# A decode-step kernel whose last weight rows come mid-run: w2's seventh rows in 13 transfers to three DMA engines' partitions, the residual by one product, w2's rest in four parts

## The chip, the cores and the metric

The kernel runs on one core of a Trainium2 chip. A core has a matrix engine (PE, whose weight loads the profile lists apart as PEld), a vector engine (DVE), an activation engine (ACT), a general engine (POOL) and a queue engine (SP) that here only issues transfers. Sixteen DMA engines move data between the memory of the chip (HBM) and the core's buffer of 128 partitions. Each engine runs its own list of instructions in order and waits where an operand is not ready.

The metric is the device time of one execution in microseconds (us), the median of several runs. Lower is better.

## What is computed

One decode step for a batch of 8: a layer norm of x, attention with a key and value cache of 8192 positions, and beside it a dense layer with the Mish activation. Both results and x are added. All numbers are float32.

```python
xn = _layernorm(x)
# attention: 32 query heads, 8 key/value heads of 128, 8 x 8192 positions
q = (xn @ wq) ...
scores = einsum("bhqd,bhkd->bhqk", q, k) * (Dh ** -0.5)
o = einsum("bhqk,bhkd->bhqd", softmax(scores), v)
att = o @ wo
# dense layer: 512 -> 1792 -> 512
h = xn @ w1 + b1
act = h * tanh(softplus(h))
ffn = act @ w2
return x + att + ffn
```

The two caches are 537 MB of the 561 MB that are read, so nearly all of the work is to bring them in once.

## The kernel before

**Units.** The work is cut into 32 units, j = 0 to 31. Unit j = 8m + b holds batch element b and the pair m of key/value heads. Its keys (kT) and its values (v) are one transfer of 8 MB each, 64 KB to each of the 128 partitions. For each unit the program writes, in this order: `scores(j)` (64 products of PE into the bank S), `softmax(j)`, `values(j - 1)` (64 products into the bank O with the values of the unit before), and `turn(j)`, which turns the exponentials of unit j into the weights `pt8` that `values(j)` reads. Unit 0 also holds `mish`, the whole first half of the dense layer: 32 + 4 passes of PE, then a row of DVE instructions that ends with the activations `aT` (lines 418 to 468). They are read only at the very end.

**Places in the buffer.** One tile `kv` holds all that streams in. Values come to its first 16384 columns (V_AT). Keys come by turns to K_AT[0] = 16384 and K_AT[1] = 24576, both 16384 columns long, so that the second half of the one place is the first half of the other. The keys of unit j + 1 can therefore start once unit j is done with the half that both share; `scores` takes that half first (argument `first`), and the load of the next keys is written between its two halves (line 558). The first weight w1 and everything that `mish` works on lie in K_AT[0] as well, so that the keys of unit 2 (line 558, in unit 1) have to wait for both: the end of `mish`, and the first half of the scores of unit 1, whose keys lie in K_AT[1]. The values of unit 1 have to wait for `values(0)`.

**Order.** The program sets the order by hand: each engine runs its instructions in the order in which the program writes them. All large transfers are issued by SP. SP waits for the place to be free, issues, and goes on to the next one. The query weights wq (four transfers of 2 MB into the tile `ws`) come between: the first at the start, the others in units 4, 12 and 20. From the end of unit 23 on `ws` has no other use than the residual: POOL loads x into its first 128 columns as `xres`, in 16 transfers of two rows each, in units 23 to 30 (line 544).

**The end.** After the last values come four transfers of wo (2 MB each, line 592) and w2 in three parts, 2 MB, 1 MB and 512 KB (line 603). A row of w2_rows belongs to one partition and holds seven pieces of 1024 columns; the parts are the pieces 0 to 3, 4 and 5, and 6. PE adds wo's products (`outputs`) and the first part's (`down_wide`) into the bank A, four groups of rows for four slices of the work; ACT copies A to the buffer (line 615); the parts two and three go to the bank H (`down`), and four products with `bsel` (line 618) add up A's four groups into H as well. DVE adds `xres` (line 627), and SP stores the result.

Of the kernel before, what the change touches and what calls it, by code (L numbers as in the profile page):

```python
# [24 lines left out]
G = 4  # L25
NH = 2
TG = SK // (NH * G) // P
BW = 1024
# [4 lines left out]
Q = P // G  # L33
# [17 lines left out]
W2R = 7  # L51
# [12 lines left out]

LOAD_Q, MAKE_Q, SPREAD_Q = 4, 5, 7

CUTS = tuple((g, lo, lo + 2) for g in range(G) for lo in range(0, B, 2))


@with_exitstack  # L70
def kernel(
# [21 lines left out]
    ws = const.tile([P, CC * BW], F32, name="ws")  # L93
# [13 lines left out]
    lsum = const.tile([P, B, H2], F32, name="lsum")  # L107
# [16 lines left out]
    qsel = const.tile([P, P], F32, name="qsel")  # L124
    oW = const.tile([P, NP, WOR, 2, B], F32, name="oW")
    qr = const.tile([P, DI, H2 * B], F32, name="qr")
    xres = ws[:, :P]
    oT = const.tile([P, 2, H2, B], F32, name="oT")
    aT = const.tile([P, 2 * W2R, B], F32, name="aT")
    pt8 = const.tile([P, HALF, PL * TL, H2], F32, name="pt8")  # L130
# [18 lines left out]
    x_sb, xc, sq = (low[:, i * D : (i + 1) * D] for i in range(3))  # L149
# [13 lines left out]
    for d in range(2):  # L163
        nc.vector.tensor_copy(
            perm.rearrange("p (d k c h) -> p d k c h", d=2, c=2, h=REP)[:, d],
            ident.rearrange("p (c d k h) -> p d k c h", c=2, d=2, h=REP)[:, d],
        )
    nc.vector.reduce_sum(
        gsum, ident.rearrange("p (x g q) -> p g x q", g=4, q=PP), axis=AX.XY
    )  # L170
# [5 lines left out]
    for d in range(2):  # L176
# [3 lines left out]
            axis=AX.XY,  # L180
# [39 lines left out]
    nc.vector.tensor_scalar(st[:, 6:7], st[:, 7:8], -0.5, 1.5, op0=ALU.mult, op1=ALU.add)  # L220
    nc.vector.tensor_mul(st[:, 4:5], st[:, 6:7], st[:, 5:6])
    nc.vector.tensor_scalar(xc, xc, st[:, 4:5], None, op0=ALU.mult)
    for c in range(CC):
        nc.tensor.transpose(M[:, c * B : (c + 1) * B], xc[:, c::CC], ident[:B, :B])
    nc.vector.tensor_copy(xn4.rearrange("p c b -> p (c b)"), M[:, 0:32])
# [192 lines left out]
    def mish(w1_t, b1_sb, flat):  # L418
        hp = H[:, :FG]
        for i in range(W1R):  # L420
            for n in range(2):
                nc.tensor.matmul(  # L422
                    hp[Q * n : Q * n + 2 * B, :],
                    xnT[:, i].rearrange("p h b -> p (h b)"),
                    w1_t[:, i, n * FG : (n + 1) * FG],
                    start=(i == 0),
                    stop=False,
                )
        for n in range(2):
# [24 lines left out]
        act = one  # L454
        half = FG // 2
        for e in range(2):
            nc.vector.tensor_mul(
                act.rearrange("p (i a e l) -> p e a l i", a=2, e=2, i=W2R)[:, e],
                h[:, half * e : half * (e + 1)].rearrange("p (a l i) -> p a l i", a=2, i=W2R),
                t1[:, half * e : half * (e + 1)].rearrange("p (a l i) -> p a l i", a=2, i=W2R),  # L460
            )
        turned = flat[:, 5 * FG : 6 * FG]
        nc.vector.transpose(turned, act)
        for h in range(2):
            nc.vector.tensor_copy(
                aT[64 * h : 64 * (h + 1)],
                turned[:64].rearrange("p (j q) -> p j q", q=Q)[:, :, h * B : (h + 1) * B],
            )


    TURN = {}

    def turn_masked(m):

        nc.vector.tensor_mul(oT[:, m % 2], oT[:, m % 2], rt.rearrange("p b h -> p h b"))
        om = TURN[m] = work.tile([P, 512], F32, name="e")[:, : WOR * H2 * B]
        nc.vector.tensor_mul(
# [18 lines left out]
    def outputs(m, t):  # L496
        w = t.rearrange("p (i h f) -> p i h f", i=WOR, h=2)
        for h in range(2):
            for i in range(WOR):
                nc.tensor.matmul(  # L500
                    A[Q * i : Q * i + B, :],
                    oW[:, m, i, h, :],
                    w[:, i, h],
                    start=(m == 0 and h == 0),
                    stop=False,
                )

    def down_wide(lo, hi, w):
        for j in range(2 * lo, 2 * hi):
            at = (j - 2 * lo) * D  # L510
            nc.tensor.matmul(
                A[Q * (j % G) : Q * (j % G) + B, :],
                aT[:, j, :],
                w[:, at : at + D],
                start=False,
                stop=(j >= 2 * hi - G),
            )

    def down(lo, hi, w, first):
        for j in range(2 * lo, 2 * hi):  # L520
            for g in range(G):
                at = (j - 2 * lo) * D + g * P
                nc.tensor.matmul(  # L523
                    H[Q * g : Q * g + B, :P],
                    aT[:, j, :],
                    w[:, at : at + P],
                    start=(first and j == 2 * lo),
                    stop=(j == 2 * W2R - 1),
                )


# [7 lines left out]
    spread()  # L539
    key_weights(0)  # L540

    def residual(g, lo, hi):

        nc.gpsimd.dma_start(  # L544
            xres[Q * g + lo : Q * g + hi, :], x[lo:hi, g * P : (g + 1) * P]
        )

    v_t = {}
    for j in range(UNITS):
        b = j % B  # L550
# [12 lines left out]
        spreads = more and b == SPREAD_Q  # L563
        if j + 1 < UNITS and not spreads:
            key_weights(j + 1)
        if j > 0:
            os = values(j - 1, v_t.pop(j - 1))
        late = j // B - 1 if b == 1 and j > B else None
        if late is not None:
            turn_masked(late)  # L570
        if j + 1 < UNITS:
            v_t[j] = load_unit(v, j, V_AT)
            if spreads:
                spread()
                key_weights(j + 1)
        for cut in CUTS[2 * (j - 23) : 2 * (j - 22)] if j >= 23 else ():
            residual(*cut)
        if j == 0:
            mish(w1_t, b1_sb, kv[:, W1_AT : W1_AT + 6 * FG])
        if more and b == LOAD_Q:  # L580
            load_q(j // B + 1)
        if more and b == MAKE_Q:
            qT = project(j // B + 1)
            mask_queries(qT)
        turn(j, late)
        if j > 0:
            merge(j - 1, os)
# [3 lines left out]
    for m in range(NP):  # L591
# [3 lines left out]
            .rearrange("u p f -> (u p f)")  # L595
            .rearrange("(p f) -> p f", p=P),
        )
    w2_rows = w2.rearrange("j p f -> (j p) f").rearrange("(q i) f -> q (i f)", i=W2R)
    w2_t = []
    parts = ((0, 4), (4, 6), (6, 7))  # L600
    for lo, hi in parts:
        t = kv[:, W2_AT + lo * BW : W2_AT + hi * BW]
        nc.sync.dma_start(t, w2_rows[:, lo * BW : hi * BW])
# [7 lines left out]
    turn_rows(NP - 1)  # L611
    outputs(NP - 1, w_o[NP - 1])
    down_wide(*parts[0], w2_t[0])
    a_sb = work.tile([P, 512], F32, name="e")
    nc.scalar.copy(a_sb, A)
    down(*parts[1], w2_t[1], True)
    for g in range(G):
        nc.tensor.matmul(
            H[Q * g : Q * g + B, :P],
# [47 lines left out]
```

## Time and profile before

| | |
|---|---|
| median of 3 runs | 1312.17 us (1312.1 to 1312.31) |
| the profiled execution | 1313.53 us, of which the profile shows a span of 1310.3 us |
| read from HBM | 561.03 MB, 428 GB/s over the span |
| PE busy | 907.7 us (69%) |
| DVE busy | 407.4 us (31%) |
| ACT and POOL busy | 41.8 us (3%) and 10.1 us (1%) |
| mean granted PE clock | 0.848 |

Times in the profile are counted from the start of the span. A page of the profile gives the busy time of each engine, then the span in 40 slices, then the DMA queues, then the chain of waits that ended last, followed back from the end. Other views list the instructions in order of time ("timeline": start, duration, engine, line, operation, and in brackets how long the engine stood idle before it and what ended that), the busy time in chosen stretches ("windows"), and the transfers with the time from issue to landing. "L314" is line 314 of the kernel; `x64` is a group of 64 instructions, and a float32 product of PE is two passes, so that 32 products show as 64.

### The profile page before, as it was taken

The page shows a single profiled execution, that of the slowest core. Times are in us where ns is not written, and L with a number is a line of the kernel's source. Part 1 is how long each engine was busy: PE and PEld are TensorE (multiplying, and loading weights), DVE is VectorE, ACT ScalarE, POOL GpSimd, SP SyncE. Part 2 cuts the span into 40 slices and gives each one's busy share as a digit, 9 for nine tenths or more (in the row PEclk, how much of TensorE's full clock was granted, in tenths as well). Part 3 has the DMA queues.
Part 4 walks back from the last instruction along what each step waited for, and adds up shares of the span by engine and source line. Part 5 has one row for each costly group of instructions (what it writes and reads, how often), then busy time and mean ns, then how long its engine had stood idle before and what let it go on. Part 6 is the DMA issues. An engine that isn't in the chain of part 4 may idle for free.

```text
span 1310.3 us, 10389 instructions
## 1 busy us (share of the span) xinstructions
PE 907.7 (69%) x4568; PEld 269.2 (21%) x4568; DVE 407.4 (31%) x881; ACT 41.8 (3%) x96; POOL 10.1 (1%) x24
## 2 busy tenths in 40 slices
PE   4967866768767567777668766687576668657667
PEld 1212221212212112222112212122121112212112
DVE  3363132331333333123331332322233331233330
ACT  1000000000000000000000000000000000000000
POOL 0000000000000000000000000011000000000000
PEclk9979887888888888887798788798887898887788
DMA  9999999999999999999999999999999999999997
GB/s 404 444 427 437 431 433 427 437 440 431 433 431 435 425 441 425 441 426 439 429 433 433 431 437 425 444 421 441 425 437 433 435 429 437 431 436 427 437 417 312
DMA packets 11668, 561.75 MB, mean 429 GB/s; under 512 B 1724, under 2 KB 1888, under 8 KB 2024
## 3 DMA queue, kind: packets, MB, share of 16 engines
q1 hardware_dynamic: 11088, 561.06, 99.2%
q8 instruction: 35, 0.57, 0.2%
q0 software_dynamic: 512, 0.02, 0.0%
q10 hardware_dynamic: 24, 0.02, 0.0%
q14 instruction: 9, 0.07, 0.0%
HBM read 561.03 MB, written 0.07 MB: 428 GB/s over the span
## 4 chain that ended last, share of the span: by engine, by line
DMA 73%; PE 23%; DVE 2%; ACT 0%; issue 0%; SPq 0%; DVEq 0%
DMA kv<-in_v 71%; PE o L393 20%; DMA kv<-in_w 3%; PE s L314 1%; PE h L250 1%; PE h L422 0%; DVE kv L452 0%; DVE tr L363 0%; PE h L523 0%; DVE wk L297 0%; DVE pt L379 0%; DVE y L373 0%; DVE nm L326 0%; ACT L216 0%; DVE ws L270 0%
## 5 line engine op out<-in xcount | busy, mean ns | idle before, releaser
L314 PE MATMUL s<-kv,wk 128*64 128x512 f32 x2048 | 512.9, 665 | 247.5 <-DMA kv<-in_kT 244.8
L393 PE MATMUL o<-kv,pt 128*32 128x512 f32 x2048 | 269.6, 686 | 46.5 <-DMA kv<-in_v 46.5
L314 PEld LDWEIGHTS s<-kv,wk 128*64 128x64 f32 x2048 | 157.5, 154 | 583.1 <-issue 327.3
L326 DVE TENSOR_REDUCE nm<-s 128x1 f32<-128x512 f32 x32 | 22.1, 692 | 547.7 <-PE s L314 547.7
L393 PEld LDWEIGHTS o<-kv,pt 128*32 128x32 f32 x2048 | 70.4, 123 | 219.5 <-issue 178.8
L363 DVE STREAM_TRANSPOSE tr<-x 128x512 f32<-128x512 f32 x128 | 79.8, 681 | 0.1
L401 DVE TENSOR_SCALAR os<-o,isel 128x128 f32<-128x128 f32 x32 | 11.2, 351 | 220.2 <-PE o L393 220.2
L297 DVE TENSOR_TENSOR wk<-qr,mask 128x512 f32<-128x512 f32 x64 | 62.5, 1019 | 5.7 <-ACT qr L286 5.7
L379 DVE SCALAR_TENSOR_TENSOR pt<-tr,gsum,y 64x256 f32<-64x256 f32 x128 | 56.2, 478 | 1.7
L345 ACT ACTIVATE e<-s,nmx 128x512 f32<-128x512 f32 x32 | 22.0, 688 | 1053.1 <-DVE nmx L342 1053.1
L373 DVE SCALAR_TENSOR_TENSOR y<-tr,gsum,y 128x512 f32<-128x512 f32 x64 | 48.4, 756 | 2.3
L350 PE MATMUL x<-e,perm 128*128 128x512 f32 x64 | 36.0, 644 | 0.0
L403 DVE SCALAR_TENSOR_TENSOR os<-o,isel,os 128x128 f32<-128x128 f32 x96 | 33.7, 351 | 3.4
L250 PE MATMUL h<-ws,xn 128*8 128x512 f32 x64 | 31.7, 642 | 0.0
L327 PE MATMUL m<-ident,nm 128*1 128x128 f32 x32 | 8.7, 273 | 29.3 <-DVE nm L326 29.3
L410 PE MATMUL m<-ident,os 128*128 128x128 f32 x32 | 10.3, 323 | 22.2 <-DVE os L403 12.2
L371 DVE TENSOR_SCALAR y<-tr,gsum 128x512 f32<-128x512 f32 x32 | 24.1, 754 | 1.1
L338 PE MATMUL m<-ident,nx 1*128 1x1 f32 x32 | 7.0, 219 | 24.1 <-DVE nx L334 24.1
L346 DVE TENSOR_SCALAR lsum<-rsel,l 128x8 f32<-128x8 f32 x32 | 7.4, 231 | 30.3 <-ACT e L345 30.3
L544 POOL DMA_DIRECT2D ws<-in_x x16 | 8.4, 527 | 901.9 <-PE h L250 870.8
L331 DVE TENSOR_REDUCE nr<-m 1x4 f32<-1x64 f32 x64 | 11.0, 207 | 11.7 <-PE m L327 11.7
L350 PEld LDWEIGHTS x<-e,perm 128*128 128x128 f32 x64 | 9.5, 188 | 23.7 <-issue 21.7
(107 smaller groups left out, 152.7 us busy)
## 6 DMA issues: line engine op xcount, KB each, us to landing
ws<-in_wq SPq DMA_DIRECT2D x4, 2048.0 KB, 34.3
kv<-in_wo SPq DMA_DIRECT2D x4, 2048.0 KB, 24.2
kv<-in_w SPq DMA_DIRECT2D x1, 3584.0 KB, 22.1
kv<-in_w SPq DMA_DIRECT2D x1, 2048.0 KB, 34.7
kv<-in_w SPq DMA_DIRECT2D x1, 1024.0 KB, 36.7
kv<-in_kT SPq DMA_DIRECT2D x32, 29.8
kv<-in_v SPq DMA_DIRECT2D x32, 30.1
kv<-in_w SPq DMA_DIRECT2D x1, 512.0 KB, 37.4
```

Of the source, the lines that this page charges most:

```text
L250: nc.tensor.matmul(H[:B, :], xn4[:, c, :], w[:, c, d * 512 : (d + 1) * 512], start=(c == 0), stop=(c == CC - 1),)
L297: nc.vector.tensor_mul(w[:, :, d], q[:, :, d].to_broadcast([P, DI, NH * G, REP]), mask[:, d * NH * G : (d + 1) * NH * G] .rearrange("p (o ...
L314: nc.tensor.matmul(S[64 * c : 64 * (c + 1), :], w[:, i].rearrange("p d k h -> p (d k h)"), kk[:, i, c, :], start=(part == 0 and n == 0), s ...
L326: nc.vector.tensor_reduce(nm, S, axis=AX.X, op=ALU.max, negate=True)
L345: nc.scalar.activation(e, S, AF.Exp, bias=nmx, accum_out=l)
L350: nc.tensor.matmul(X, perm, e, start=True, stop=True)
L363: nc.vector.transpose(tr.rearrange("p (l t) c -> p t l c", t=TL)[:, tl], X.rearrange("p (t o q l) -> p t l o q", t=TL, o=1, q=PP)[:, tl].t ...
L371: nc.vector.tensor_scalar(y, kinds[:, 0], gsum[:, 0:1], None, op0=ALU.mult)
L373: nc.vector.scalar_tensor_tensor(y, kinds[:, g], gsum[:, g : g + 1], y, op0=ALU.mult, op1=ALU.add)
L379: nc.vector.scalar_tensor_tensor(pt8[half, c, :, d * REP : (d + 1) * REP], kinds[half, 3, :, c * REP : (c + 1) * REP], gsum[half, 3:4], y[ ...
L393: nc.tensor.matmul(O[Q * q : Q * (q + 1), :], pt8[:, c, TL * l : TL * (l + 1), :].rearrange("p t h -> p (t h)"), vt[:, 512 * n : 512 * (n ...
L403: nc.vector.scalar_tensor_tensor(os, O[:, DH * i : DH * (i + 1)], isel[:, i : i + 1], os, op0=ALU.mult, op1=ALU.add)
```

## The change

w2's pieces 0 to 5 still come at the end, now in four parts: 1 MB, 1 MB, 512 KB, 512 KB. The seventh piece (`late_rows`, 128 rows of 4 KB) comes mid-run through ACT's queue into `ws`, in 13 transfers: five in units 16 to 18, eight in units 24 to 27. Twelve of them have three rows of partitions as their outer dimension (partition p, p + 4 and p + 8, with two or four pieces of 4 KB to each), 120 of the 128 rows in all; the thirteenth brings the last 8 rows to eight partitions. Since several rows of w2 now lie in one partition, the activations that belong to them have to be moved to those partitions: `deal_early` does it right behind `mish` in unit 0, with a mask `kmask` and one product with a selection matrix `esel`, into the new tile `aE`. `early_products` multiplies them in units 19 and 29 into the bank A. The residual is now a product of the identity with x at the start, the first one into A; the 16 POOL transfers are gone. Line numbers of the changed kernel are those of the diff's new side, 80 more at the end.

```diff
+LEAD, LS, LK = 3, 4, 4
+SPAN, SLOTS = LEAD * LS, LK + 2
+LATE = 2 * SPAN * LK
+REST = LATE + 2 * SPAN
+EARLY_AT = {16: (8, 10), 17: (10, 12), 18: (12, 13), 24: (0, 2), 25: (2, 4), 26: (4, 6), 27: (6, 8)}
+PRODUCE_AT = {19: (LK, SLOTS, 2 * Q), 29: (0, LK, Q + SPAN)}
...
-    xres = ws[:, :P]
+    esel = const.tile([P, 2 * Q], F32, name="esel")
+    kmask = const.tile([P, SLOTS], F32, name="kmask")
+    aE = const.tile([2 * Q, SLOTS, 2, B], F32, name="aE")
...
+    nc.vector.memset(esel, 0.0)
+    for u in range(2):
+        nc.vector.reduce_sum(
+            esel[:, Q * u : Q * u + SPAN].rearrange("p (e s) -> p e s", e=LEAD),
...
+    nc.vector.tensor_add(kmask[:, LK : LK + 1], kmask[:, LK : LK + 1], lsum[:, 0, :1])
     nc.vector.reduce_sum(
         gsum, ident.rearrange("p (x g q) -> p g x q", g=4, q=PP), axis=AX.XY
...
+    nc.tensor.matmul(A[:B, :], ident[:B, :B], x_sb, start=True, stop=False)
...
+    def deal_early():
+
+        last = work.tile([P, 512], F32, name="e")[:, : SLOTS * 2 * B]
+        nc.vector.tensor_mul(
+            last.rearrange("p (k c) -> p k c", k=SLOTS),
+            aT[:, 2 * W2R - 2 :]
+            .rearrange("p (o e) b -> p o (e b)", o=1)
+            .to_broadcast([P, SLOTS, 2 * B]),
+            kmask.rearrange("p (k o) -> p k o", o=1).to_broadcast([P, SLOTS, 2 * B]),
+        )
+        nc.tensor.matmul(
+            M[: 2 * Q, 192 : 192 + SLOTS * 2 * B], esel, last, start=True, stop=True
+        )
+        nc.scalar.copy(
+            aE.rearrange("p k e b -> p (k e b)"),
+            M[: 2 * Q, 192 : 192 + SLOTS * 2 * B],
+        )
...
-    def residual(g, lo, hi):
-
-        nc.gpsimd.dma_start(
-            xres[Q * g + lo : Q * g + hi, :], x[lo:hi, g * P : (g + 1) * P]
-        )
+    w2_rows = w2.rearrange("j p f -> (j p) f").rearrange("(q i) f -> q (i f)", i=W2R)
+    late_rows = w2_rows[:, (W2R - 1) * BW :]
+
+    def early(n):
+
+        if n < 2 * LS:
+            ks, (u, s), q = LK, divmod(n, LS), n * LK * LEAD
+        else:
+            ks, u, s = 2, 0, n - 2 * LS
+            q = LATE + s * ks * LEAD
+        if n < 3 * LS:
+            p = Q * u + s
+            rows = slice(p, p + (LEAD - 1) * LS + 1, LS)
+            nc.scalar.dma_start(
+                ws[rows, : ks * BW].rearrange("e (k f) -> e k f", k=ks),
+                late_rows[q : q + ks * LEAD].rearrange("(k e) f -> e k f", e=LEAD),
+            )
+        else:
+            nc.scalar.dma_start(ws[Q : 2 * Q : LS, :BW], late_rows[REST:])
+
+    def early_products(lo, hi, rows):
+
+        for n in range(2 * lo, 2 * hi):
+            k, e = divmod(n, 2)
+            at = (n - 2 * lo) * D
+            nc.tensor.matmul(
+                A[Q * (n % G) : Q * (n % G) + B, :],
+                aE[:rows, k, e],
+                ws[:rows, at : at + D],
+                start=(lo > 0 and n % G > 0),
+                stop=False,
+            )
...
-        for cut in CUTS[2 * (j - 23) : 2 * (j - 22)] if j >= 23 else ():
-            residual(*cut)
+        if j in PRODUCE_AT:
+            early_products(*PRODUCE_AT[j])
+        for n in range(*EARLY_AT.get(j, (0,))):
+            early(n)
         if j == 0:
             mish(w1_t, b1_sb, kv[:, W1_AT : W1_AT + 6 * FG])
+            deal_early()
...
-    parts = ((0, 4), (4, 6), (6, 7))
+    parts = ((0, 2), (2, 4), (4, 5), (5, 6))
...
     down_wide(*parts[0], w2_t[0])
+    down_wide(*parts[1], w2_t[1])
     a_sb = work.tile([P, 512], F32, name="e")
     nc.scalar.copy(a_sb, A)
-    down(*parts[1], w2_t[1], True)
+    down(*parts[2], w2_t[2], True)
...
-    down(*parts[2], w2_t[2], False)
+    down(*parts[3], w2_t[3], False)
     res = work.tile([P, DH], F32, name="os", bufs=1)
-    nc.vector.tensor_add(res, H[:, :P], xres)
+    nc.vector.tensor_copy(res, H[:, :P])
```

PE around units 0 and 1, before: `s` are the scores, `m` the transposes of the softmax, `h` the products of `mish`, `x` the first product of `turn(0)`.

```order
L314 MATMUL s<-kv,wk 64x512 x32
L327 MATMUL m<-ident,nm 1x128
L338 MATMUL m<-ident,nx 128x1
L422 MATMUL h<-kv 16x448 x16
L430 MATMUL h<-kv 16x448 x2
L350 MATMUL x<-e,perm 128x512
L314 MATMUL s<-kv,wk 64x512 x32
```

The same place in the changed program:

```order
L346 MATMUL s<-kv,wk 64x512 x32
L359 MATMUL m<-ident,nm 1x128
L370 MATMUL m<-ident,nx 128x1
L454 MATMUL h<-kv 16x448 x16
L462 MATMUL h<-kv 16x448 x2
L513 MATMUL m<-e,esel 64x96
L382 MATMUL x<-e,perm 128x512
L346 MATMUL s<-kv,wk 64x512 x32
```

One product stands between the last product of `mish` and the scores of unit 1; its operand `e` is written by the DVE row below. DVE at the end of `mish` in the changed program (`kv` is the work space of `mish`, `tr`, `y` and `pt_99` belong to `turn(0)`):

```order
L484 RECIPROCAL kv<-kv 128x448
L485 TENSOR_TENSOR kv<-kv 128x448
L489 TENSOR_TENSOR kv<-kv 128x2x16x7 x2
L495 STREAM_TRANSPOSE kv<-kv 128x448
L497 COPY aT<-kv 64x112 x2
L506 TENSOR_TENSOR e<-aT,kmask 128x96
L395 STREAM_TRANSPOSE tr<-x 128x16x32 x4
```

Only L506 is new there, behind the copy to `aT`; at the head of DVE's list ten instructions for `esel` and `kmask` are new, ahead of the other constants. PE at the end of the program, before (`a` and `h` are the banks A and H):

```order
L500 MATMUL a<-kv,oW 8x512 x8
L511 MATMUL a<-kv,aT 8x512 x8
L523 MATMUL h<-kv,aT 8x128 x16
L618 MATMUL h<-e,bsel 8x128 x4
L523 MATMUL h<-kv,aT 8x128 x8
```

and in the changed program, where half of the first group of H's products is gone:

```order
L550 MATMUL a<-kv,oW 8x512 x8
L561 MATMUL a<-kv,aT 8x512 x8
L573 MATMUL h<-kv,aT 8x128 x8
L698 MATMUL h<-e,bsel 8x128 x4
L573 MATMUL h<-kv,aT 8x128 x8
```

More of the change, by code (lines that the diff above doesn't have):

```diff
@@ L65 @@
 LOAD_Q, MAKE_Q, SPREAD_Q = 4, 5, 7
-CUTS = tuple((g, lo, lo + 2) for g in range(G) for lo in range(0, B, 2))
+LEAD, LS, LK = 3, 4, 4
[4 more added lines that the diff above has]
+PRODUCE_AT = {19: (LK, SLOTS, 2 * Q), 29: (0, LK, Q + SPAN)}
 @with_exitstack
@@ L167 @@
         )
+    nc.vector.memset(esel, 0.0)
+    for u in range(2):
+        nc.vector.reduce_sum(
+            esel[:, Q * u : Q * u + SPAN].rearrange("p (e s) -> p e s", e=LEAD),
+            ident[:, :LATE].rearrange("p (u s k e) -> p u e s k", u=2, s=LS, k=LK)[:, u],
+            axis=AX.X,
+        )
+    sums = lsum.rearrange("p b h -> p (b h)")[:, :SPAN]
+    nc.vector.reduce_sum(
+        sums.rearrange("p (e s) -> p e s", e=LEAD),
+        ident[:, LATE:REST].rearrange("p (s k e) -> p e s k", s=LS, k=2),
+        axis=AX.X,
+    )
+    nc.vector.tensor_add(esel[:, :SPAN], esel[:, :SPAN], sums)
+    nc.vector.tensor_add(esel[:, Q::LS], esel[:, Q::LS], ident[:, REST:])
+    for at, lo, hi in ((0, 0, LATE), (LK, LATE, REST)):
+        ks = LK if at == 0 else 2
+        nc.vector.reduce_sum(
+            kmask[:, at : at + ks],
+            ident[:, lo:hi].rearrange("p (x k e) -> p k x e", k=ks, e=LEAD),
+            axis=AX.XY,
+        )
+    nc.vector.reduce_sum(lsum[:, 0, :1], ident[:, REST:], axis=AX.X)
+    nc.vector.tensor_add(kmask[:, LK : LK + 1], kmask[:, LK : LK + 1], lsum[:, 0, :1])
     nc.vector.reduce_sum(
@@ L468, in mish @@
             )
+    def deal_early():
[13 more added lines that the diff above has]
+            M[: 2 * Q, 192 : 192 + SLOTS * 2 * B],
+        )
     TURN = {}
@@ L503, in outputs @@
                     w[:, i, h],
-                    start=(m == 0 and h == 0),
+                    start=False,
                     stop=False,
@@ L515, in down_wide @@
                 start=False,
-                stop=(j >= 2 * hi - G),
+                stop=(j >= 2 * parts[2][0] - G),
             )
@@ L527, in down @@
                     start=(first and j == 2 * lo),
-                    stop=(j == 2 * W2R - 1),
+                    stop=(j == 2 * W2R - 3),
                 )
@@ L540 @@
     key_weights(0)
-    def residual(g, lo, hi):
-        nc.gpsimd.dma_start(
-            xres[Q * g + lo : Q * g + hi, :], x[lo:hi, g * P : (g + 1) * P]
-        )
+    w2_rows = w2.rearrange("j p f -> (j p) f").rearrange("(q i) f -> q (i f)", i=W2R)
[12 more added lines that the diff above has]
+                late_rows[q : q + ks * LEAD].rearrange("(k e) f -> e k f", e=LEAD),
+            )
+        else:
[10 more added lines that the diff above has]
+                stop=False,
+            )
     v_t = {}
@@ L597 @@
         )
-    w2_rows = w2.rearrange("j p f -> (j p) f").rearrange("(q i) f -> q (i f)", i=W2R)
     w2_t = []
-    parts = ((0, 4), (4, 6), (6, 7))
+    parts = ((0, 2), (2, 4), (4, 5), (5, 6))
     for lo, hi in parts:
```

## The prediction

> **What bounds the kernel now.** First the page: the slices of the span, the queues, the chain.
>
> ```profile
> DMA  9999999999999999999999999999999999999997
> DMA packets 11668, 561.75 MB, mean 429 GB/s; under 512 B 1724, under 2 KB 1888, under 8 KB 2024
> q1 hardware_dynamic: 11088, 561.06, 99.2%
> q8 instruction: 35, 0.57, 0.2%
> ...
> DMA 73%; PE 23%; DVE 2%; ACT 0%; issue 0%; SPq 0%; DVEq 0%
> ```
>
> The sixteen DMA engines are busy from the first slice to the last but one. Every byte of caches and weights passes once, at 429 GB/s. PE stands in the chain, but always in turn with a transfer that was queued long before, so making PE faster or slower moves nothing until SP issues a transfer too late. So three things set the time: whether the stream ever runs dry, which DMA engine ends last, and what follows the last byte.
>
> The end, in the view by windows (PE, PEld, DVE, ACT, POOL busy, PE clock, DMA share, GB/s):
>
> ```profile
> 1297.00:1298.00 1.00, 0.59 (x8) 0.23 (x12) 0.12 (x1) 0.20 (x1) 0.00 (x0) 1.00 1.01 422
> 1298.00:1303.00 5.00, 2.17 (x24) 0.34 (x16) 0.00 (x0) 0.00 (x0) 0.00 (x0) 1.00 0.55 233
> ...
> 1304.00:1305.00 1.00, 0.92 (x13) 0.28 (x13) 0.00 (x0) 0.37 (x1) 0.00 (x0) 0.50 0.20 82
> ```
>
> The share falls from 1.01 to 0.55 at 1298 and stays there for five us: 9 of 16 is 0.56. Seven engines are done; nine go on, the last to about 1305.4. Each had the same number of bytes. The single packets of the trace, put into chains (each starts as the one ahead ends), say why: a code load of PE (35 on q8, one per 37 us) holds one engine up by some 1.5 us, and they go round among the nine late ones.
>
> **The stall that I expect.** The new product with `esel` (L513 of the change) reads what DVE makes of `aT`, the last result of `mish`. PE runs in order, and behind this product stand unit 0's first product of `turn`, all scores of unit 1 and `values(0)`. Rows of the timeline of before:
>
> ```profile
> 48.22 0.33 SPq L141 DMA_DIRECT2D kv<-in_v  x1
> ...
> 57.12 1.13 PE L350 MATMUL x<-e,perm 128*128 128x512 f32 x2
> ...
> 58.18 13.95 PE L314 MATMUL s<-kv,wk 128*64 128x512 f32 x64
> ...
> 68.74 0.44 DVE L465 COPY aT<-kv 64x112 f32<-64x112 f32 x2
> ...
> 69.25 0.33 SPq L141 DMA_DIRECT2D kv<-in_kT  x1
> ...
> 76.00 0.69 DVE L326 TENSOR_REDUCE nm<-s 128x1 f32<-128x512 f32 x1
> ...
> 78.06 8.73 PE L393 MATMUL o<-kv,pt 128*32 128x512 f32 x64
> ...
> 95.63 15.37 PE L314 MATMUL s<-kv,wk 128*64 128x512 f32 x64 [6.87 <-DMA kv<-in_kT]
> 104.17 0.33 SPq L141 DMA_DIRECT2D kv<-in_kT  x1
> ```
>
> In before PE starts unit 1's scores at 58.18, beside `mish` on DVE. SP issues unit 2's keys at 69.25, when `aT` is done; the first half of the scores, for which they also wait, had long ended. In the change both stand in one row. Step by step:
>
> ```profile
> 3.08 0.28 DVE L168 TENSOR_REDUCE gsum<-ident 128x4 f32<-128x128 f32 x1
> ...
> 6.08 0.67 DVE L209 TENSOR_REDUCE st<-kv 8x1 f32<-8x512 f32 x1
> ...
> 402.74 0.43 DVE L477 TENSOR_TENSOR e<-oT,usel 128x256 f32<-128x256 f32 x1
> 403.22 0.70 PE L487 MATMUL m<-e,qsel 128*128 128x256 f32 x2 [1.23 <-DVE e L477]
> ```
>
> - Ten more DVE constants stand ahead of the norm of x. Fourteen small ones take 3.08 to 6.08, so 0.21 each: 2.1 us. The way from there to `aT` is one chain (norm, queries, key weights, scores 0, `mish`), so `aT` comes at 71.3, not 69.2.
> - Mask product on DVE 0.3, new product 0.4 (their likes above, twice as wide and more, take 0.43 and 0.70), L350 1.2: the scores of unit 1 start at 73.2, fifteen us later.
> - Their first half takes 7.0 (half of 13.95) if PE runs warm, 8.5 (95.63 to 104.17, where SP waited for just this) after an idle gap. I take 7.9. SP can issue unit 2's keys at 81.1.
>
> ```profile
> 95.00:97.00 2.00, 1.37 (x4) 0.53 (x6) 0.29 (x1) 0.00 (x0) 0.00 (x0) 0.50 1.21 524
> ...
> 99.00:101.00 2.00, 2.00 (x12) 0.60 (x10) 0.00 (x0) 0.00 (x0) 0.00 (x0) 1.00 0.98 426
> ```
>
> After 6.9 us without work the granted clock was 0.50 here and 1.00 again from 99. The gap in the change is 12 us, so the same is due; the product and L350 use up some of the slow time, hence 7.9. The Trainium skill, "TensorE: Matmul & The Clock Gate", section "What's actually happening", says that half speed comes after an idle window of about 3.4 us and ends after as much sustained work. This trace agrees; by that rule the first half is an estimated 7.0 + (3.4 - 1.6) / 2 = 7.9 as well, since the product and L350 fill 1.6 of the slow time, and the sum below stays; with a PE that stayed warm it would be 0.9 lower.
>
> Does the stream last that long? The values of unit 0 were issued at 48.22, in time, and 2 us later still are. Unit 2's keys land in before at 95.6 (L314 waits for them); 8.39 MB at 429 GB/s is 19.55 us, and some 0.4 goes from the last byte to the waiting engine: so the data ahead of them end at 75.6. The packet chains give each engine's end of unit 0's values, 73.8 to 75.7, most within 0.8 us of the first. A start from nothing costs more:
>
> ```profile
> 0.74 0.37 SPq L135 DMA_DIRECT2D ws<-in_wq  x1
> 0.74:6.00 5.26, 0.00 (x0) 0.00 (x0) 4.84 (x19) 1.28 (x1) 1.52 (x4) 1.00 0.82 279
> ```
>
> From the first issue to 6.00 the mean was 279 of 429 GB/s: as if 5.26 x (1 - 279/429) = 1.8 us were lost. So data flow again as from 82.9, and the engines stand still for 7.2 (the one that ended last) to 9.1 us (the first). A standstill sets them all level, so what counts is the gap of those that end the run. By the chains these are three that carry five code loads, and two of them were done at 73.8 and 74.3: **8.7 us lost** (bounds 5.5 and 10.5: constants 1.4 to 2.6, half 7.0 to 8.5, start 1.1 to 2.5, which engine).
>
> Is unit 1's values' issue late too? It follows `values(0)`: scores end at 73.2 + 14.8 = 88.0, the softmax needs 2.1 more (DVE at 76.00, L393 at 78.06 in before), 8.7 for the products: 98.9. The keys' data last to 82.9 + 19.55 = 102.5. In time, by 1.8 us after the start-up.
>
> **The seventh piece.** 120 of 128 rows go through three engines: 40 x 4 KB each.
>
> ```profile
> q10 hardware_dynamic: 24, 0.02, 0.0%
> L314 PE MATMUL s<-kv,wk 128*64 128x512 f32 x2048 | 512.9, 665 | 247.5 <-DMA kv<-in_kT 244.8
> ```
>
> q10's 24 packets are x (8 rows) and b1 (4 rows), each with a data and a completion packet: as many engines as outer rows. At 429 / 16 = 26.8 GB/s the 164 KB cost 6.1 us on each of three engines, in place of 1.2 of their share at the end. By the chains the four that carried b1 are among the seven early ones, as far as neighbours can be told apart. Five code loads of 1.5 after the standstill put the seven 7 us ahead again; they pay 6.1 + 0.2 - 1.2 = 5.1 and still end first. So this piece costs nothing and takes its 512 KB off the end. PE's twelve products (24 passes) in units 19 and 29 lie in the 247.5 us, some 8 per unit, that it waits for keys; ACT's issues lie on an engine busy 3%. PE waits there for transfers issued at least one unit (39 us) before.
>
> The Trainium skill, "DMA: Bandwidth & Descriptors", "Rules for kernel authors", advises the opposite, an outermost dimension that uses all 16 engines; its section "Why a DMA increments its semaphore by 16 and not by 1" lets three rows take the three lowest-numbered engines. The first is the rule against this change and a rival below; the packets agree with the second for 8 and 4 rows.
>
> **The end.**
>
> ```profile
> kv<-in_w SPq DMA_DIRECT2D x1, 1024.0 KB, 36.7
> kv<-in_w SPq DMA_DIRECT2D x1, 512.0 KB, 37.4
> 1267.42 1.38 SPq L603 DMA_DIRECT2D kv<-in_w  x3
> 1304.61 1.90 PE L523 MATMUL h<-kv,aT 128*8 128x128 f32 x32
> 1306.28 0.65 PE L618 MATMUL h<-e,bsel 128*8 128x128 f32 x8
> 1306.70 0.68 PE L523 MATMUL h<-kv,aT 128*8 128x128 f32 x16
> ```
>
> Issued some 0.5 us apart, the last two parts land at 1304.6 and 1305.8: the last 512 KB are worth **1.2 us**. PE ends at 1307.4, 1.6 after the last landing, because the 32 passes of part two start at 1304.6. In the change part three has 16: 0.95 from a landing 1.2 ahead of the last, 0.45 for L618, then 0.5 to 0.7 for the last group, so PE ends 0.8 after it: **0.8 us** gained (0.4 to 1.2). The 16 POOL transfers go:
>
> ```profile
> q0 software_dynamic: 512, 0.02, 0.0%
> ```
>
> Their share shows as 0.0%; the chains slow by 0.2 us in all over units 23 to 30. I take **0.2** (0 to 0.4).
>
> **Sum.** 8.7 - 1.2 - 0.8 - 0.2 = +6.5. Against the profiled execution (1313.53, its span 1310.3 and 3.2 around it) that is 1320.0; it stood 1.36 over the median, so 1312.17 + 6.5 = **1318.7**. Two runs of this kernel that differ by under 0.2% (2.6 us) can't be told apart.
>
> **Rivals.**
> - *PE's wait doesn't reach the queue.* What decides: SP must issue unit 2's keys by 73.7, so unit 1's scores must start by 66. For it speaks that the queue is 6 us deep at that place; against it that `aT` alone ends at 69.2 already in before. Then only 1.2 + 0.8 + 0.2 remain: 1310.0, the other side of the forecast. 7%.
> - *Keys in time, values late.* If unit 2's keys don't need the first half of unit 1's scores, they go at 71.3, their data end at 95, and only unit 1's values (98.9 + 1.8) come late: 6 us, 1316. The two places share half their columns, which speaks against it. 6%.
> - *The three engines aren't early ones*, as the skill's advice would have it: each then ends 5.1 later rather than 1.2 earlier: 1318.7 + 6.1 = 1324.8. Against it stand the chains. 6%.
> - *The change doesn't do what it says*: all 120 rows go through one engine, 18.3 us on one that is 7 ahead, about 1329. 3%.
>
> **How the numbers follow.** The forecast has 78%, its own range 1315.6 to 1321 from the bounds above. With the second rival inside it, 1315.5 to 1321.2 holds 8 in 10. Slower by over 0.2% (above 1314.8): 0.91; within 0.2%: 0.06 (most of the first rival); faster: 0.03.
>
> **What would show it.** In the profile of the change PE idles 12 us before L513, released by DVE; the scores of unit 1 start near 73 and SP's issue of unit 2's keys stands near 81, where before it stood at 69. The windows between 74 and 84 show a DMA share near 0; this happens once. At the end the share of the engines falls later and more evenly, from a lead of the seven that three of them have spent, and the last products start within 0.5 us of the last landing. It is wrong if the share has no hole near 80, if a second hole follows near 102, or if three engines run on alone at the end.

## The result and the profile after

| | before | changed |
|---|---|---|
| median of the runs compared | 1311.87 us (1311.32 to 1312.31, 6 runs) | 1319.85 us (1317.89 to 1321.89, 6 runs) |
| ratio, 95% interval | 1 | 1.0059 (1.0049 to 1.0070) |
| profiled execution, its span | 1313.53, 1310.3 | 1319.84, 1318.1 |

The change makes the kernel 8.0 us slower. The page of the changed kernel, the slices, the queues and the chain:

```profile
DMA  9979999999999999999999999999999999999997
GB/s 402 440 319 422 436 442 422 436 436 430 432 430 430 440 428 438 428 432 436 424 445 423 435 437 434 426 437 426 436 438 425 437 426 439 435 430 426 440 420 328
DMA packets 11473, 561.75 MB, mean 426 GB/s; under 512 B 1304, under 2 KB 1436, under 8 KB 1828
...
q10 hardware_dynamic: 196, 0.55, 0.1%
...
DMA 73%; PE 24%; DVE 2%; issue 0%; ACT 0%; SPq 0%
```

The third slice, 66 to 99 us, is the only one inside the run whose digit falls below 9: 319 GB/s where its neighbours have 422 and more. One slice is 33 us, so (1 - 319/429) x 33 = 8.5 us of stream are missing there. The chain at the foot hardly differs from before: a hole of 8 us is half a per cent of it. The timeline around the hole (start, duration, engine, line, operation, idle time before):

```profile
49.56 0.33 SPq L148 DMA_DIRECT2D kv<-in_v  x1
...
70.04 0.44 DVE L497 COPY aT<-kv 64x112 f32<-64x112 f32 x2
70.51 0.26 DVE L506 TENSOR_TENSOR e<-aT,kmask 128x96 f32<-128x96 f32 x1
70.83 0.58 PE L513 MATMUL m<-e,esel 128*64 128x96 f32 x2 [12.29 <-DVE e L506]
71.34 2.08 PE L382 MATMUL x<-e,perm 128*128 128x512 f32 x2
...
73.34 15.28 PE L346 MATMUL s<-kv,wk 128*64 128x512 f32 x64
...
81.79 0.33 SPq L148 DMA_DIRECT2D kv<-in_kT  x1
...
97.81 0.33 SPq L148 DMA_DIRECT2D kv<-in_v  x1
...
104.79 16.61 PE L346 MATMUL s<-kv,wk 128*64 128x512 f32 x64 [5.07 <-DMA kv<-in_kT]
```

PE idles 12.29 us before L513, until DVE has written `e`. The scores of unit 1 begin at 73.34, where before they began at 58.18, and SP issues unit 2's keys at 81.79 in place of 69.25. The windows over that place (PE, PEld, DVE, ACT and POOL busy, PE clock, DMA share, GB/s):

```profile
70.00:75.00 5.00, 4.17 (x8) 1.32 (x10) 2.24 (x7) 0.23 (x1) 0.00 (x0) 0.50 0.55 236
75.00:80.00 5.00, 5.00 (x24) 1.70 (x22) 4.78 (x9) 0.00 (x0) 0.00 (x0) 0.90 0.00 0
80.00:85.00 5.00, 5.00 (x26) 1.58 (x24) 0.21 (x1) 0.00 (x0) 0.00 (x0) 1.00 0.62 210
85.00:90.00 5.00, 3.89 (x19) 1.08 (x15) 0.88 (x3) 0.00 (x0) 0.00 (x0) 1.00 0.97 419
```

The same place in before, which has no gap:

```profile
75.00:80.00 5.00, 2.50 (x14) 0.85 (x18) 3.19 (x11) 0.78 (x2) 0.00 (x0) 0.50 0.97 419
```

In the changed kernel no transfer starts between 75 and 80. Against 429 GB/s the four windows lack 2.2 + 5.0 + 2.6 + 0.1 = 9.9 us of stream. A window counts a packet of 2.4 us whole, by its start, so the edges of windows and slice blur both figures: 8.5 and 9.9 are two rough readings of one loss. No second hole follows: unit 1's values, issued at 97.81, still reach a busy queue. The last stretch, by windows and by the timeline:

```profile
1304.00:1306.00 2.00, 0.70 (x2) 0.30 (x2) 0.90 (x4) 0.20 (x1) 0.00 (x0) 1.00 0.86 356
1306.00:1308.00 2.00, 1.49 (x16) 0.34 (x16) 0.21 (x1) 0.20 (x1) 0.00 (x0) 1.00 0.80 334
1308.00:1310.00 2.00, 1.45 (x12) 0.12 (x8) 0.00 (x0) 0.00 (x0) 0.00 (x0) 1.00 0.73 305
1310.00:1312.00 2.00, 0.72 (x8) 0.12 (x8) 0.00 (x0) 0.00 (x0) 0.00 (x0) 0.92 0.72 295
1312.00:1314.00 2.00, 2.00 (x32) 0.89 (x32) 0.00 (x0) 0.59 (x1) 0.00 (x0) 0.50 0.10 39
```
```profile
1312.60 1.10 PE L573 MATMUL h<-kv,aT 128*8 128x128 f32 x16
...
1313.59 0.61 PE L698 MATMUL h<-e,bsel 128*8 128x128 f32 x8
1313.98 1.08 PE L573 MATMUL h<-kv,aT 128*8 128x128 f32 x16
1315.12 0.29 DVE L707 COPY os<-h 128x128 f32<-128x128 f32 x1 [8.91 <-PE h L573]
```

Where before the share dropped to 0.55 and stayed there, it now drops to 0.73 and stays there until 1312: twelve engines of sixteen (12/16 is 0.75) in place of nine. By the packet records nine transfers were in flight at a time from 1299 to 1303 in before, and twelve are from 1307 to 1311 here, so three of the seven early engines now end with the late ones. PE's last products, though, run at a granted clock of 0.50.

### The profile page after: what moved, and what is told of

Its sections match the earlier page's. It is cut to its first block, busy times and chain, and to the rows that moved or that the text cites. A ratio compares the mean times of both kernels' runs of the same rounds, so it can differ in the third digit from the quotient of the medians.

```text
span 1318.1 us, 10423 instructions
## 1 busy us (share of the span) xinstructions
PE 908.6 (69%) x4580; PEld 268.9 (20%) x4580; DVE 408.3 (31%) x892; ACT 42.0 (3%) x97; POOL 1.7 (0%) x8
## 4 chain that ended last, share of the span: by engine, by line
DMA 73%; PE 24%; DVE 2%; issue 0%; ACT 0%; SPq 0%
DMA kv<-in_v 70%; PE o L425 19%; DMA kv<-in_w 3%; PE s L346 2%; PE h L282 1%; PE h L454 0%; DVE kv L484 0%; PE x L382 0%; DVE wk L329 0%; PE h L573 0%; PE a L561 0%; DVE nm L358 0%; ACT L247 0%; DVE ws L302 0%; ACT e L290 0%
## 5 line engine op out<-in xcount | busy, mean ns | idle before, releaser
L425 PE MATMUL o<-kv,pt 128*32 128x512 f32 x2048 | 262.4, 671 | 45.4 <-DMA kv<-in_v 45.4
L382 PE MATMUL x<-e,perm 128*128 128x512 f32 x64 | 36.9, 659 | 0.0
L382 PEld LDWEIGHTS x<-e,perm 128*128 128x128 f32 x64 | 9.7, 191 | 23.2 <-issue 21.2
```

The lines of the kernel that those rows point to most:

```text
L382: nc.tensor.matmul(X, perm, e, start=True, stop=True)
L425: nc.tensor.matmul(O[Q * q : Q * (q + 1), :], pt8[:, c, TL * l : TL * (l + 1), :].rearrange("p t h -> p (t h)"), vt[:, 512 * n : 512 * (n ...
```

## The experiments

Each ratio is against the kernel before on the same chip. The medians of before there were 1312.1 us in all three groups of runs, so the groups can be laid side by side.

### Where the dealing stands

**deal_late**: the dealing behind unit 1's scores in place of ahead of them.

```diff
         if j == 0:
             mish(w1_t, b1_sb, kv[:, W1_AT : W1_AT + 6 * FG])
+        if j == 1:
             deal_early()
```

> The changed kernel with the dealing of the last activations (mask product on DVE, product with the selection matrix on PE, copy on ACT) written in unit 1, behind its scores, instead of in unit 0 ahead of them. Nothing else moves. Theory (PE's wait in front of unit 1's scores makes SP issue unit 2's keys too late, and the DMA engines stand still): the keys are issued near 71 us again, the DMA share has no hole between 75 and 84, and the time falls by about 9.5 us from the changed kernel's 1319.9 to 1310.3 (1309 to 1311.5), a little below before. Rival 1 (the 13 transfers on three engines make the stream longer): it stays at 1317 or more. Rival 2 (the end in four parts costs it): it stays at 1317 or more as well, with the loss after 1300 us.

Measured: 1309.99 us (1309.89 to 1311.08, 11 runs), ratio 0.9985 (0.9976 to 0.9994). The issue is early again and the hole is gone:

```profile
69.92 0.33 SPq L148 DMA_DIRECT2D kv<-in_kT  x1
...
75.00:80.00 5.00, 1.84 (x10) 0.66 (x14) 3.25 (x12) 0.78 (x2) 0.00 (x0) 0.75 0.97 419
```

**deal_between** leaves the mask product in unit 0 and puts the product with `esel` between the two halves of unit 1's scores:

```diff
             k_t[j + 1] = load_unit(kT, j + 1, K_AT[(j + 1) % 2])
+        if j == 1:
+            deal_product(dealt)
         scores(j, k, j % 2 == 0, 1)
...
             mish(w1_t, b1_sb, kv[:, W1_AT : W1_AT + 6 * FG])
-            deal_early()
+            dealt = deal_mask()
```

> The changed kernel with the mask product still behind the end of mish in unit 0, but PE's product with the selection matrix between the two halves of unit 1's scores. PE waits for aT as long as before, until about 71 us, only with less behind it: the first half of the scores, for which unit 2's keys wait, is then done. Theory (it matters what stands behind the waiting product, not the wait): unit 2's keys are issued near 71, unit 1's values near 90, no hole, 1310.3 (1309 to 1312) as in the run with the dealing in unit 1. Rival (PE's wait of 5 us costs by itself, or unit 1's values become late): a smaller hole near 95 us, 1313 to 1316.

Measured: 1310.29 us (1309.79 to 1311.63, 10 runs), ratio 0.9987 (0.9978 to 0.9996). Its timeline:

```profile
60.01 7.09 PE L346 MATMUL s<-kv,wk 128*64 128x512 f32 x32
70.53 0.44 DVE L497 COPY aT<-kv 64x112 f32<-64x112 f32 x2
71.00 0.26 DVE L506 TENSOR_TENSOR e<-aT,kmask 128x96 f32<-128x96 f32 x1
71.04 0.33 SPq L148 DMA_DIRECT2D kv<-in_kT  x1
71.32 0.42 PE L517 MATMUL m<-e,esel 128*64 128x96 f32 x1 [4.22 <-DVE e L506]
```

PE waits for `aT` here too, 4.22 us, but behind the half that SP waits for: SP issues at 71.04 and the stream goes on. So a wait of PE for DVE costs nothing by itself. The whole loss comes from what stood behind it.

**before_deal** is the other half of the argument: the kernel before with the constants and the dealing alone, whose result nothing reads.

```diff
             mish(w1_t, b1_sb, kv[:, W1_AT : W1_AT + 6 * FG])
+            deal_early()
```

> The kernel before with one part of the change alone: the ten constants and the dealing in unit 0, ahead of unit 1's scores. Its result is used by nothing; the residual, the end and all transfers are as before. Theory: the hole in the stream is there in full, 8.7 us in the sum (9.3 if the changed kernel's 8 us and its savings of 1.2 and 0.2 are added up): 1311.9 + 9 = 1320.9 (1319 to 1322.5). Rivals 1 and 2 (transfers or end to blame): 1312 to 1313.

Measured: 1320.29 us (1319.30 to 1322.30, 5 runs), ratio 1.0065 (1.0053 to 1.0078), +8.2 us. The late issue and the hole are there:

```profile
80.74 0.33 SPq L148 DMA_DIRECT2D kv<-in_kT  x1
...
75.00:80.00 5.00, 5.00 (x26) 1.63 (x24) 4.30 (x8) 0.00 (x0) 0.00 (x0) 1.00 0.00 0
80.00:85.00 5.00, 5.00 (x26) 1.68 (x24) 0.00 (x0) 0.00 (x0) 0.00 (x0) 1.00 0.81 301
```

**after_delay**: is the loss as long as the delay? Two more reciprocals, whose results nobody reads, between `aT` and the mask product of the changed kernel.

```diff
+            flat = kv[:, W1_AT : W1_AT + 6 * FG]
+            for _ in range(2):
+                nc.vector.reciprocal(flat[:, FG : 2 * FG], flat[:, 4 * FG : 5 * FG])
             deal_early()
```

> The changed kernel with two more reciprocals, whose results nobody reads, on DVE between aT and the mask product, 2.95 us each by the row of L484, so 5.9 us in all. Theory (the path mask product, selection product, first half of unit 1's scores, issue of unit 2's keys is late as a whole, and the DMA engines stand still for each us of it): 1319.9 + 5.9 = 1325.8 us, SP's issue at 87.7 in place of 81.8. Rival (the 8 us are not from this wait alone, or are made up later by queued transfers): less than 3 us slower than the changed kernel.

Measured: 1326.50 us (1325.10 to 1326.97, 4 runs), ratio 1.0107 (1.0091 to 1.0122), +6.6 us over the changed kernel, its span +6.4.

```profile
71.17 5.94 DVE L661 RECIPROCAL kv<-kv 128x448 f32<-128x448 f32 x2
77.02 0.20 DVE L506 TENSOR_TENSOR e<-aT,kmask 128x96 f32<-128x96 f32 x1
...
88.80 0.33 SPq L148 DMA_DIRECT2D kv<-in_kT  x1
```

The mask product comes 6.5 us later than in the changed kernel (aT also ended 0.7 later in this run), the issue 7.0, by the packet records the last data 7.2 (1320.47 and 1313.24), the end 6.4. Past the point where the queue is empty the time goes up one for one with the delay.

### The seventh piece and the three engines

**spread16**: no dealing and no constants; the seventh piece by one transfer of 128 rows to 128 partitions in unit 24, multiplied by `aT` in unit 29.

```diff
+        nc.scalar.dma_start(ws[:, :BW], late_rows)
...
+                A[Q * n : Q * n + B, :],
+                aT[:, j, :],
+                ws[:, n * D : (n + 1) * D],
+                start=(n == 1),
```

> The changed kernel without the dealing and its constants; w2's seventh piece comes by one transfer of 128 rows, 4 KB to each partition, so over all sixteen DMA engines, in unit 24, and is multiplied by aT as it is, in unit 29. The end in four parts stays. So every engine carries its 32 KB mid-run in place of at the end. Theory (the three engines that took the piece were ahead and paid with idle time; worth one sixteenth of 512 KB each, 1.2 us): 1.2 us slower than the kernel that deals in unit 1 (1310.0 us), so 1311.2, and at most 1 us faster than before. Rival (which engines carry the piece does not matter; the gain of that kernel is from the end alone): 1310.0, the same as that kernel.

Measured: 1311.30 us (1311.15 to 1312.52, 11 runs), ratio 0.9995 (0.9986 to 1.0004), 1.3 us over deal_late. Its windows at the end:

```profile
1298.00:1300.00 2.00, 1.26 (x12) 0.34 (x16) 0.22 (x1) 0.40 (x2) 0.00 (x0) 1.00 0.67 279
1300.00:1302.00 2.00, 1.58 (x16) 0.12 (x8) 0.00 (x0) 0.00 (x0) 0.00 (x0) 1.00 0.56 236
1302.00:1304.00 2.00, 0.58 (x12) 0.12 (x8) 0.00 (x0) 0.00 (x0) 0.00 (x0) 1.00 0.53 217
```

The plateau of before is back at 0.56 and 0.53: seven engines have ended and nine go on. That 1.3 us is what three early engines are worth, 1.2 by the bytes.

How much of their lead is left? Four kernels send some of the thirteen transfers a second time, so that the three engines carry more. No result depends on the second copies.

**late_dup**: eight of them in units 24 to 27, to partitions 16 to 27 and 48 to 59.

```diff
+            p = Q * u + 16 + s
...
+        if 24 <= j < 28:
+            for n in range(2 * (j - 24), 2 * (j - 24) + 2):
+                early_again(n)
```

> The kernel that deals in unit 1 (1310.0 us), with eight of the thirteen transfers issued a second time in units 24 to 27, to partitions whose contents change no result: 32 more packets of 4 KB on each of the three engines, at 26.8 GB/s 4.9 us each. Theory (the three engines had 6 to 8 us of lead and have about 1 us left): 4 us slower, 1314 us, and at the end three engines run on alone. Rival (the three engines are still far ahead, or small transfers cost less than their bytes): within 1 us of 1310.0.

Measured: 1319.29 us (1318.68 to 1319.57, 5 runs), ratio 1.0053 (1.0040 to 1.0066): +9.3 us, more than twice what the theory gave, for 4.9 us of bytes. At the end three engines do run on alone, as expected: the share falls to 0.22 (3/16 is 0.19), and from 1311.5 to 1313 three packets are in flight at a time.

```profile
1308.00:1310.00 2.00, 1.57 (x19) 0.12 (x8) 0.00 (x0) 0.00 (x0) 0.00 (x0) 1.00 0.47 195
1310.00:1312.00 2.00, 0.63 (x8) 0.12 (x8) 0.00 (x0) 0.00 (x0) 0.00 (x0) 1.00 0.22 90
```

So the next three ask whether it is their number or their density, to partitions 64 to 75 and 96 to 107, beside the kernel that deals in unit 1 (**late_again**):

```diff
+            p = 64 + Q * u + s
...
+        if 28 <= j < 30:
+            for n in range(2 * (j - 28), 2 * (j - 28) + 2):
+                early_again(n)
```

This is **late_add4**; **late_add8** goes on to unit 31; **late_add8x** has four each in units 28 and 29.

> The kernel that deals in unit 1, once more, as the measure for the three kernels beside it on the same chip: 1310.0 us.

> The kernel that deals in unit 1, with four of the thirteen transfers issued a second time, two each in units 28 and 29, to partitions that no product reads: 16 packets of 4 KB more on each of the three engines, by 0.16 us each 2.6 us. Theory (of their lead of 7 us the three engines have spent 5.1 and have 1.9 left): 0.7 us slower, 1310.7. Rival (nothing left): 2.6 us slower. Second rival (still far ahead): no change, 1310.0.

> The same with eight transfers, two each in units 28 to 31: 32 packets, 5.1 us more on each of the three engines. Theory: 3.2 us slower, 1313.2. Rival (nothing left): 5.1 us slower, 1315.1. Second rival (still far ahead): no change. Third (what cost 9 us in the kernel with the second issue in units 24 to 27 comes with every further transfer, since the packets of all sixteen engines took longer there): 9 us slower, 1319.

> The same eight transfers, but four each in units 28 and 29, as dense as in units 24 to 27 of the kernel that took 1319.3. Theory (the bytes on the three engines decide, not how densely they come): as with two per unit, within 0.5 us. Rival (four per unit slow the packets of all sixteen engines): slower than with two per unit by 2 us or more, with stretches in which the packets of 64 KB take about 2.6 us in place of 2.42.

| | median us (lowest to highest, runs) | ratio, 95% interval | over late_again |
|---|---|---|---|
| late_again | 1310.03 (1309.71 to 1310.80, 11) | 0.9986 (0.9978 to 0.9995) | |
| late_add4 | 1314.49 (1313.96 to 1315.16, 11) | 1.0019 (1.0010 to 1.0028) | 4.5 |
| late_add8 | 1319.43 (1319.15 to 1320.36, 5) | 1.0059 (1.0045 to 1.0072) | 9.4 |
| late_add8x | 1319.22 (1318.80 to 1319.89, 5) | 1.0057 (1.0045 to 1.0070) | 9.2 |

Density doesn't matter. Each transfer costs 1.1 to 1.2 us, but by its bytes it would cost 0.64 (4 packets x 0.16 us on each engine). Windows of 40 us, of late_again and then of late_add8, show where the rest is:

```profile
1140.00:1180.00 40.00, 24.43 (x134) 7.44 (x134) 12.34 (x28) 1.56 (x4) 0.00 (x0) 0.87 1.00 433
1180.00:1220.00 40.00, 29.48 (x153) 8.51 (x157) 11.95 (x26) 0.78 (x2) 0.00 (x0) 0.81 1.01 435
```
```profile
1140.00:1180.00 40.00, 26.11 (x132) 7.67 (x132) 11.02 (x22) 0.78 (x2) 0.00 (x0) 0.83 1.00 419
1180.00:1220.00 40.00, 27.58 (x148) 8.01 (x148) 11.08 (x25) 0.78 (x2) 0.00 (x0) 0.83 0.99 413
```

The share of busy engines is the same, and yet they move less: their packets take longer. The packet records give the figure:

```
packets of 64 KB that take 2.44 to 2.85 us (2.42 is usual), their excess over 2.42 as a share of 16 engines
late_again   28 packets, 0.16 us
late_add4   261 packets, 2.5 us   stretches 1144-1166, 1185-1207
late_add8   435 packets, 4.1 us   stretches 1144-1167, 1185-1208, 1227-1249, 1268-1284
late_add8x  528 packets, 4.9 us   1144-1238
late_dup    533 packets, 5.5 us   stretches 1013-1034, 1060-1082, 1105-1130, 1152-1174
```

The slow stretches of late_add4 and late_add8 last as long as the second copies are on their way, some 20 us for two transfers, and lose 1.2 us each. Nearly nine in ten of the packets of 64 KB in them are slow (116 of 131 in the first), so they touch all sixteen engines; beside the first thirteen transfers it is one in 130 at most. With that taken off there remain 4.5 - 2.5 = 2.0 us of the 2.6 of bytes, and 5.3, 4.3 and 3.8 of the 5.1 of the others (late_dup against late_again). By this reckoning, which leans on the share taken off for the slow packets, the three engines have between nothing and 1.3 us left of their lead, less than the theory's 1.9. "Still far ahead" is out, by the three engines that run on alone too. Why second copies slow all engines when the first thirteen don't stays open: they differ in the partitions that they write and in reading rows that were read before, and no run parts these two.

### The end

**before_res**: the kernel before with the residual as one product; the 16 POOL transfers are gone.

```diff
+    nc.tensor.matmul(A[:B, :], ident[:B, :B], x_sb, start=True, stop=False)
...
-    nc.vector.tensor_add(res, H[:, :P], xres)
+    nc.vector.tensor_copy(res, H[:, :P])
```

> The kernel before with the residual by one product at the start and without the 16 POOL transfers; the end has its copy in place of the sum. Prediction's term: 0.2 us faster, 1311.7 (1311.3 to 1311.9), no difference that can be told. Rival (small transfers hold the engines up more than their share shows, as a code load does): 1 us or more faster.

Measured: 1311.78 us (1311.04 to 1312.98, 11 runs), ratio 0.9998 (0.9989 to 1.0007). No difference that can be told. Its profiled run ends at full clock:

```profile
1304.52 1.06 PE L522 MATMUL h<-kv,aT 128*8 128x128 f32 x32 [0.57 <-DMA kv<-in_w]
...
1305.75 0.62 PE L522 MATMUL h<-kv,aT 128*8 128x128 f32 x16
```

**late_parts2**: deal_late with w2's rest by two transfers, products unchanged.

```diff
-    for lo, hi in parts:
+    for lo, hi in ((0, 4), (4, 6)):
```

> The kernel that deals in unit 1 (1310.0 us), with w2's rest issued as two transfers, 2 MB and 1 MB, in place of four; the products are the same. Theory (what follows the last byte counts: the products of the 1 MB, 32 passes, can start only when all of it has landed, in place of 16 ahead and 16 behind): 0.5 to 0.9 us slower, 1310.5 to 1310.9. Rival (fewer and larger transfers make up for it, or the last products are hidden): 1310.0 or less.

Measured: 1312.06 us (1310.71 to 1313.07, 11 runs), ratio 0.9998 (0.9989 to 1.0007), 2.1 us over deal_late, where 0.5 to 0.9 was expected. The fastest runs lie 0.8 apart (1310.71 and 1309.89), as expected; the rest is scatter, 2.4 us with large parts as in before, about 1.1 with four. What makes it wasn't tried. In the four parts of the same kernel the clock makes a difference of its own. First late_again, then deal_late, the same program:

```profile
1303.38 0.62 PE L573 MATMUL h<-kv,aT 128*8 128x128 f32 x16 [0.21 <-DMA kv<-in_w]
1303.94 0.40 PE L699 MATMUL h<-e,bsel 128*8 128x128 f32 x8
1304.61 0.62 PE L573 MATMUL h<-kv,aT 128*8 128x128 f32 x16 [0.27 <-DMA kv<-in_w]
```
```profile
1303.70 1.10 PE L573 MATMUL h<-kv,aT 128*8 128x128 f32 x16
...
1304.69 0.61 PE L699 MATMUL h<-e,bsel 128*8 128x128 f32 x8
1305.08 1.08 PE L573 MATMUL h<-kv,aT 128*8 128x128 f32 x16
```

At full clock the last products wait for the last landing and take 0.62; at half clock they no longer wait for a transfer but for PE itself, and end 0.9 later (1306.16 in deal_late, 1305.23 in late_again), of which 0.2 are later data (1304.40 and 1304.16). The profiled runs took 1311.08 and 1310.45.

## Why the prediction was right, point by point

The sign and the mechanism are shown, and the range of 1315.5 to 1321.2 held the median of 1319.85. The forecast of +6.5 was 1.5 us short of the medians' 8.0, and 1.3 short of the spans' 7.8. The profiled executions differ by 6.3, since the time around the span was 3.2 us in before's and 1.7 in this one: an agreement with +6.5 that comes from the frame, not from the sum. By its steps:

| step | predicted | measured |
|---|---|---|
| constants, `aT` done at | +2.1, 71.3 | +1.3, 70.48 |
| mask product, `esel` product, L382 | 0.3 + 0.4 + 1.2 | 0.26, 0.58, 2.08 |
| scores of unit 1 from | 73.2 | 73.34 |
| their first half, issue of unit 2's keys | 7.9, 81.1 | 8.45, 81.79 |
| stream lost at the last engine | 8.7 | 9.1 |
| unit 1's values issued | 98.9, in time | 97.81, in time |
| 512 KB off the stream, on three engines | -1.2, no other cost | -1.3 (spread16 against deal_late) |
| PE's tail | -0.8 | -0.2 |
| POOL transfers | -0.2 | not told from nothing |

- **The stall.** The place, the releaser and the length of the wait (12.29 us) are as forecast. Two misses cancel on the way to the scores: the constants cost less than by the mean of fourteen others (the norm's L240 starts at 7.42, its likeness in before at 6.08), and L382 ran at half clock for its whole length (2.08). The first half then took 8.45, nearly the cold bound of 8.5. PE ran at half clock from the first product at 70.83 to 76.0 (clock 0.50 from 75.5 to 76.0, 0.96 from 76.0 to 76.5), 5.2 us where the prediction's estimate had 3.4, so that 2.7 us of it fell into the scores in place of 1.8. Here the measurement decides.
- **The loss.** By the packet records the last data came 7.9 us later than in before (1313.24 against 1305.37), with 1.2 us of bytes less: 9.1. It follows the late issue, which came 0.7 later than forecast. The start on a dry queue was rightly taken at 1.8: the second packets of the sixteen engines start on average 1.8 us later than in a flow that began with the issue (issue plus 2.42 us), and 1.9 later in before_deal and in after_delay. The last packets ahead of the hole end at 74.4 on average, and data flow again as from 83.6: each engine stands still for 9.2 us, close to the 9.1. In before_deal the same reading gives 8.2 us, and the last data come 8.4 later than in before; in after_delay it gives 16.3, and the last data come 15.1 later with 1.2 us of bytes less. So the 0.4 over the forecast is, to 0.1, the issue's 0.7 less 0.2, since the engines fell idle later than forecast. That the dealing in this place is enough to make the loss is shown by before_deal (+8.2) and after_delay; that nothing else in the change makes it, by deal_late and deal_between.
- **The seventh piece.** Three early engines take it for nothing, as argued from the chains: by spread16 they are worth 1.3 us, and twelve engines in place of nine are at work near the end. They have spent nearly all of their lead on it.
- **The end.** This term was mis-sized, and its reason was wrong. "PE ends 0.8 after it" holds where PE is at full clock (late_again: the last group starts at 1304.61, just behind its landing, and takes 0.62). In the profiled run of the change the clock was 0.50, and PE ended 1.8 us after the last data (1315.06 and 1313.24), in before 2.0 (1307.38 and 1305.37), where the clock was 0.50 from 1304.6 to 1306.5. At full clock it ended 1.1 after them in late_again with four parts (1305.23 and 1304.16), and just as long after them in before_res with the three parts of before (1306.37 and 1305.28): its 32 passes took 1.06 in place of before's 1.90. So the late end that the prediction read in before came from the half clock and not from the 32 passes as such, and at like clocks the four parts are worth 0.2 us or nothing. The prediction left the clock open; whether the four parts change how often it is full isn't shown.
- The terms that were off add up: 0.4 of the loss, 0.6 of the tail and 0.2 of POOL are 1.2 of the 1.3 by which the span was missed.

Of the rivals, "PE's wait doesn't reach the queue" priced the change without the stall at 1310.0: that is what deal_late runs at. It fell here since SP's issue depends on PE's place in the program. "Keys in time, values late" and "three engines not early" fall by the timeline and by spread16, "one engine" by the shares at the end.

Two kernels beat both: dealing behind unit 1's scores (1309.99 and 1310.03) or between their halves (1310.29). The first is 2.1 us under before, 9.9 under the change.

## What to carry to other kernels

When a stream bounds the kernel, ask of every new wait not how long it is but which queued instruction behind it releases the next transfer, and how long the queue lasts at that moment; past that point each microsecond counts in full. A product that is needed a thousand microseconds later belongs behind the work that frees the buffers. Bytes given to engines that end early are free only up to their lead, so measure the lead, and measure with more load that the lead is still there.

## What the runs showed that was not expected

- Further transfers of 48 KB over three engines slowed the packets of all sixteen from 2.42 to about 2.6 us for as long as they ran (late_add4: 433 and 435 GB/s fell to 421 and 418 in two windows of 40 us), though the first thirteen did not. The cause is open.
- The same program had its last products at full clock in one profiled run and at half clock in another (0.62 and 1.10 us for L573), 0.7 us from the last data to PE's end (1.1 and 1.8). What decides it wasn't tried.
- The runs with the hole scatter more: 4.0 us over 6 runs of the change and 3.0 over 5 of before_deal, against 1.2 and 1.1 over 11 of the kernel that deals late. Nothing here says why.
